# FFT convolution and two expert layers on one core: seven block products for eight in layer two's first product

## Chip, cores and metric

One core of one Trainium2 chip. The metric is the device time of one execution in microseconds. TensorE is PE in the profile (its weight loads PEld), VectorE is DVE, ScalarE ACT, GpSimd POOL, and SP is the engine that issues most DMAs.

## The reference

```python
X = np.fft.rfft(x, axis=1)                                  # x: (2, 3008, 256)
y = np.fft.irfft(X * (filt_r + 1j * filt_i)[None], n=3008, axis=1)
x = y.reshape(6016, 256)
h = x @ moe_w_in                                            # 256 -> 2048
x = np.where(h > 0, h, np.exp(np.minimum(h, 0)) - 1) @ moe_w_out     # 2048 -> 256
h = x @ moe2_w_in
return (h * np.clip(h + 3, 0, 6) / 6) @ moe2_w_out
```

The weights come as 64-bit floats, everything else in 32 bits.

## The kernel before, in words

Features lie on partitions and tokens along the free axis. The convolution is made of small Fourier matrices on PE: for the first sequence ahead of everything else, for the second in between the units of layer one (`PROLOGUE`, `s1`, `mid`, `i1`).

The two layers then work in **units** (layer, token block, hidden block): 12 token blocks of 512, 512, 512, 512, 480 and 480 tokens per sequence, and 16 hidden blocks of 128. A unit has two products. The first (`g1`) goes from 256 features, two blocks of 128, to 128 hidden values; the second (`g2`) goes from those to 256 outputs, two blocks of 128 in two PSUM banks that add up over the 16 hidden blocks. Each product of a 128x128 weight block with a token block is done three times by `mm3` (lines 78 to 81): operands are split in a high part, rounded to fp32r, and the rest, and high by rest, rest by high and high by high are added up in PSUM. So a unit is 4 x 3 = 12 matmuls. Splitting is `split` (lines 74 to 76): an ACT copy (L75) and a DVE subtraction (L76). Between the two products of a layer-two unit stand an ACT relu (L347), a DVE gate (L348) and a split; in layer one it is L341, L342 and L343 and a split.

The loop at lines 587 to 599 is the order of the program: for each unit n first `pre[n]`, then `g1` of unit n, the split of unit n-1, `g2` of unit n-3, and `post[n]`. Units 0 to 191 are layer one, 192 to 383 layer two. `pre` and `post` hold all the side work: the second sequence's convolution, the making of layer two's weights from their 64-bit words (`w_chain`, units 100 to 179, written to memory as `scrw`), and their loading into the buffers of layer one's weights as these come free (`w_load`, on POOL's queue, from unit 179 on). All engines run their queues in order. Layer one's outputs stay in SBUF as `x2`, in the pool `p4` of twenty 4 KB tiles, and are split by `x_split` four units ahead of use. The pool `p2` has twenty 2 KB tiles, PSUM eight banks.

Of the kernel before, what the change touches and what calls it, by code (L numbers as in the profile page):

```python
# [42 lines left out]
def fft_conv_moe_moe2(ctx, tc, xp, fq, sg, cs1, cs1t, cs2, ci2, ci1, ident, w1i, w1o, w2i, w2o, out):  # L43
# [273 lines left out]

    xs, x2, gs, outs = {}, {}, {}, {}

    def x_split(layer, blk, h):  # L320
# [361 lines left out]
```

## Time and profile before

| | |
|---|---|
| median of 3 runs | 1153.73 us (1153.63 to 1154.84) |
| profiled execution | 1154.02 us, of which the span from first to last instruction is 1152.3 us |
| PE, PEld busy | 1136.1 us, 942.7 us |
| DVE, ACT, POOL busy | 760.1 us, 695.7 us, 73.7 us |
| chain that ended last | PE 92% of the span |
| granted TensorE clock | 1.00 |

Busy time of PE counts overlapping matmuls once, and a matmul's duration reaches over the start of the next one. The start of one to the start of the next is what a matmul costs in a stream. For ACT and DVE the same holds on a smaller scale.

### The profile page before, as it was taken

What the parts mean: (1) busy time and instruction counts of PE and PEld (TensorE: products, weight loads), DVE (VectorE), ACT (ScalarE), POOL (GpSimd) and SP (SyncE); (2) the same over time, 40 slices, a digit from 0 to 9 for tenths busy, and PEclk for the clock granted to TensorE, in tenths of its full rate; (3) what the DMA queues carried; (4) which work ended last, traced back from release to release, by engine and by line L of the source; (5) the groups of instructions that cost most, each with busy time, mean ns of one, the idle gap of its engine ahead of it and who ended that gap; (6) DMA issues with size and microseconds to landing.
All of it is one profiled execution on the core that took longest, in us unless ns stands there. A gap on an engine that the chain in (4) does not pass through costs nothing.

```text
span 1152.3 us, 13760 instructions
## 1 busy us (share of the span) xinstructions
PE 1136.1 (99%) x5212; PEld 942.7 (82%) x5212; DVE 760.1 (66%) x1206; ACT 695.7 (60%) x1237; POOL 73.7 (6%) x69
## 2 busy tenths in 40 slices
PE   8899999999999999999999999999999999999998
PEld 5588888788788888888888888888888888888887
DVE  6989998679963788787875555455455555455553
ACT  3477777876676777777776444444444444444443
POOL 3600000024310000000002000000000000000000
PEclk9999999999999999999999999999999999999999
DMA  9991100354522122222226100000000000000000
GB/s 290 290 300 65 42 1 1 110 160 148 165 74 72 37 74 73 74 74 73 81 84 202 54 19 1 19 19 1 19 18 1 18 19 1 19 19 1 19 18 18
DMA packets 50019, 79.75 MB, mean 69 GB/s; under 512 B 4000, under 2 KB 32544, under 8 KB 49952
## 3 DMA queue, kind: packets, MB, share of 16 engines
q1 hardware_dynamic: 46672, 70.14, 19.1%
q0 software_dynamic: 2304, 8.39, 2.4%
q8 instruction: 41, 0.67, 0.2%
q10 hardware_dynamic: 976, 0.34, 0.1%
q14 instruction: 26, 0.21, 0.1%
HBM read 54.87 MB, written 23.99 MB: 68 GB/s over the span
## 4 chain that ended last, share of the span: by engine, by line
PE 92%; DMA 4%; DVE 2%; ACT 0%; SPq 0%; issue 0%; POOL 0%; ACTq 0%; POOLq 0%; DVEq 0%
PE ps L79 30%; PE ps L81 30%; PE ps L80 30%; PE ps L216 2%; DMA raw<-in_w1o 1%; DMA t<-in_fq 1%; DMA t<-in_xp 1%; DVE t L190 1%; DVE t L189 1%; DMA id<-in_ident 1%; POOL t L192 0%; DVE t L76 0%; DMA t<-scr 0%; PE ps L197 0%; ACT t L75 0%
## 5 line engine op out<-in xcount | busy, mean ns | idle before, releaser
L79 PE MATMUL ps<-t,w 128*128 128x512 f32 (+1 forms) x1536 | 593.6, 386 | 0.6 <-DVE t L76 0.5
L81 PE MATMUL ps<-t,w 128*128 128x512 f32 (+1 forms) x1536 | 592.2, 386 | 0.0
L80 PE MATMUL ps<-t,w 128*128 128x512 f32 (+1 forms) x1536 | 592.1, 385 | 0.0
L76 DVE TENSOR_TENSOR t<-t,t 128x512 fp32r<-128x512 f32 (+2 forms) x472 | 329.0, 705 | 9.5 <-ACT t L75 7.6
L79 PEld LDWEIGHTS ps<-t,w 128*128 128x128 f32 x1536 | 288.2, 188 | 56.9 <-PE ps L81 0.9
L81 PEld LDWEIGHTS ps<-t,w 128*128 128x128 f32 x1536 | 288.2, 188 | 55.2
L80 PEld LDWEIGHTS ps<-t,w 128*128 128x128 f32 x1536 | 288.2, 188 | 54.8
L75 ACT ACTIVATE t<-t 128x512 fp32r<-128x512 f32 (+2 forms) x472 | 283.1, 611 | 24.6 <-POOL t L192 24.1
L348 DVE SCALAR_TENSOR_TENSOR t<-t,ps 128x512 f32<-128x512 f32 (+1 forms) x192 | 130.0, 677 | 250.7 <-ACT t L347 250.7
L347 ACT ACTIVATE t<-ps,three 128x512 f32<-128x512 f32 (+1 forms) x192 | 130.6, 680 | 268.6 <-PE ps L81 268.6
L343 DVE SCALAR_TENSOR_TENSOR t<-t,ps 128x512 f32<-128x512 f32 (+1 forms) x192 | 129.5, 675 | 109.3 <-ACT t L342 108.1
L341 ACT ACTIVATE t<-ps 128x512 f32<-128x512 f32 (+1 forms) x192 | 112.3, 585 | 104.5 <-PE ps L81 104.4
L342 ACT ACTIVATE t<-t 128x512 f32<-128x512 f32 (+1 forms) x192 | 119.8, 624 | 6.1
L125 POOL TENSOR_TENSOR t<-t,sg 128x512 f32<-128x512 f32 x24 | 30.3, 1265 | 191.6 <-DMA t<-in_fq 180.7
L192 POOL TENSOR_TENSOR t<-t,t 128x512 f32<-128x512 f32 x24 | 34.9, 1454 | 73.5 <-DVE t L190 48.8
L189 DVE TENSOR_TENSOR t<-ps,t 64x512 f32<-64x512 f32 x48 | 33.1, 689 | 5.7 <-POOL t L125 2.8
L216 PEld LDWEIGHTS ps<-i,t 96*128 96x128 f32 x256 | 31.3, 192 | 3.6 <-issue 2.5
L216 PE MATMUL ps<-i,t 96*128 96x94 f32 x256 | 31.1, 273 | 0.4 <-DMA t<-scr 0.4
L316 POOL DMA_DIRECT2D w<-scrw x16 | 8.6, 540 | 298.8 <-PE ps L81 298.8
L70 ACT ACTIVATE t<-ps 128x512 f32<-128x512 f32 (+12 forms) x51 | 19.4, 421 | 12.4 <-PE ps L149 8.0
L269 DVE SCALAR_TENSOR_TENSOR t<-raw,t 128x512 f32<-128x512 uint32 x32 | 22.3, 697 | 2.0
L263 DVE SCALAR_TENSOR_TENSOR t<-raw,t 128x512 uint32<-128x512 uint32 x32 | 22.7, 710 | 0.4
(54 smaller groups left out, 384.1 us busy)
## 6 DMA issues: line engine op xcount, KB each, us to landing
t<-in_fq SPq DMA_DIRECT2D x24, 512.0 KB, 6.2
scrw<-t SPq DMA_DIRECT2D x16, 512.0 KB, 3.0
w<-scrw POOLq DMA_DIRECT2D x16, 512.0 KB, 4.5
t<-in_xp SPq DMA_DIRECT2D x16, 384.0 KB, 5.2
scr<-t SPq DMA_DIRECT2D x24, 256.0 KB, 2.7
t<-scr SPq DMA_DIRECT2D x16, 384.0 KB, 5.1
raw<-in_w1i SPq DMA_DIRECT2D x18, 256.0 KB, 5.8
raw<-in_w1o SPq DMA_DIRECT2D x18, 256.0 KB, 5.7
```

The lines of the kernel that those rows point to most:

```text
L75: nc.scalar.activation(hi, src, AF.Copy)
L76: nc.vector.tensor_tensor(out=lo, in0=src, in1=_f32(hi), op=ALU.subtract)
L79: nc.tensor.matmul(acc, wh, xl, start=start, stop=False)
L80: nc.tensor.matmul(acc, wl, xh, start=False, stop=False)
L81: nc.tensor.matmul(acc, wh, xh, start=False, stop=stop)
L189: nc.vector.tensor_tensor(out=v[o], in0=acc[a], in1=flat(f[a, 1]), op=ALU.mult)
L216: nc.tensor.matmul(accs[h, jg][:, (j - jg * TG) * TJ : (j - jg * TG + 1) * TJ], vin[b, h, j // 8][:, j % 8, :], mats["i1"], start=True, st ...
L341: nc.scalar.activation(r[:, :n], acc[:, :n], AF.Relu, scale=-1.0)
L342: nc.scalar.activation(r[:, :n], r[:, :n], AF.Exp, scale=-1.0)
L343: nc.vector.scalar_tensor_tensor(out=r[:, :n], in0=r[:, :n], scalar=-1.0, in1=acc[:, :n], op0=ALU.add, op1=ALU.max)
L347: nc.scalar.activation(r[:, :n], acc[:, :n], AF.Relu, bias=three)
L348: nc.vector.scalar_tensor_tensor(out=r[:, :n], in0=r[:, :n], scalar=6.0, in1=acc[:, :n], op0=ALU.min, op1=ALU.mult)
```

## The change

Layer two's first product is taken for two token blocks and two hidden blocks at a time: a product of a 2x2 block matrix of weights (hidden block by feature block) with a 2x2 block matrix of tokens. Eight block products became seven, in Winograd's form of Strassen's scheme. A **group** (p, q) is a pair p of token blocks (six pairs) and a pair q of hidden blocks (eight, "quarters" in what follows). It makes seven products `prod` 1 to 7, each of three matmuls, and eight `second` products of three matmuls.

- The products add up in three banks a, b and c: 1 in a, 2 in b, 6 on top of a, 5 in c, 7 on a, 4 on a, 3 on c. In between ACT copies a to SBUF (`copy`: m1, u2, u3) and DVE adds a copy to a bank (`add`), which gives the hidden blocks (0,0), (1,1) and (0,1); (1,0) is a itself at the end. Then come `relu` (ACT), `gate` (DVE) and `part` (the split), partly in the next group, together with the old group's `second` products. Below, add00 is `add((0, 0))`, and hi00 and lo00 are the ACT and DVE halves of `part((0, 0))`; likewise for the others.
- The weight sums (`w_sums`) are made in layer one, each time two hidden blocks of weights are there: four POOL instructions at once; three units later an ACT copy and a POOL subtraction; five units later a DVE addition and a write to memory. `s_load` brings the sums back on POOL's queue from unit 180 on, behind `w_load`'s.
- The token sums (`x_sums`, four POOL subtractions a pair) and seven splits (`x_part`; four before) are made one pair ahead: for the first pair at units 166 to 188 of layer one, for the others in quarters 2 to 7 of the pair before.
- Layer one's outputs are written to memory (`scrx`) and loaded two blocks at a time (`x2_load`).
- At the end the last group's rest is worked off by itself.

```diff
@@ g2 @@
-        if l == 0:
-            x2[blk] = t
+        nc.sync.dma_start(scrx[blk][:, :, :n], t[:, :, :n])
@@ new: weight sums, called from w_parts for every odd hidden block @@
+    def w_sums(q):
...
+        for out, a, b, op in (
+            (s1, a21, a22, ALU.add), (s2, s1, a11, ALU.subtract),
+            (s3, a11, a21, ALU.subtract), (s4, a12, s2, ALU.subtract),
+        ):
+            nc.gpsimd.tensor_tensor(out=out, in0=a, in1=b, op=op)
...
+        def rounded():
+            nc.scalar.activation(rh, th, AF.Copy)
+            nc.gpsimd.tensor_tensor(out=th, in0=th, in1=_f32(rh), op=ALU.subtract)
+
+        def summed():
+            nc.vector.tensor_tensor(out=rl, in0=th, in1=tl, op=ALU.add)
+            nc.sync.dma_start(scrs[q], _f32(r.rearrange("p q i f -> p (q i f)")))
+
+        pre[now[0] + 3].append(rounded)
+        pre[now[0] + 5].append(summed)
@@ new: token sums and a product @@
+    def x_sums(p, i):
...
+        out, a, b = ((t1, b12, b11), (t2_, b22, t1), (t3, b22, b12), (t4_, b21, t2_))[i]
+        nc.gpsimd.tensor_tensor(out=out, in0=a, in1=b, op=ALU.subtract)
...
+    def prod(p, q, m, acc, start):
...
+        mm3(acc[:, :n], w[:, 0], w[:, 1], x[:, 0, :n], x[:, 1, :n], start, True, True)
@@ new: a group; old is the group before @@
+        a, b, c = bank(), bank(), bank()
+        prod(p, q, 1, a, True)
+        m1 = g.copy(a)
+        prod(p, q, 2, b, True)
+        g.add((0, 0), m1, b)
+        if old:
+            old.part((1, 0))
+            old.relu((0, 1))
+            old.gate((0, 1))
+            old.second((0, 0))
...
+        g.relu((0, 0))
+        if old:
+            old.part((0, 1))
+        g.gate((0, 0))
+        prod(p, q, 6, a, False)
+        u2 = g.copy(a)
+        prod(p, q, 5, c, True)
+        g.part((0, 0))
+        for fn in beside:
+            fn()
+        if old:
+            old.second((1, 1))
...
+        prod(p, q, 7, a, False)
+        u3 = g.copy(a)
+        g.add((1, 1), u3, c)
+        if old:
+            old.second((1, 0))
+            if old.q == NF // 2 - 1:
+                out_evac(old.p, 0)
...
+        g.relu((1, 1))
+        g.gate((1, 1))
+        if old:
+            old.second((0, 1), (0,))
+        prod(p, q, 4, a, False)
+        g.h[1, 0] = a
+        g.relu((1, 0))
+        if (p, q) != (5, NF // 2 - 1):
+            g.gate((1, 0))
+        if old:
+            old.second((0, 1), (1,))
...
+        g.part((1, 1))
+        prod(p, q, 3, c, False)
+        g.add((0, 1), u2, c)
+        return g
@@ the work beside the groups, by quarter; the end @@
+        ahead2 = {
+            1: [(x2_load, 0), (x2_load, 1)], 2: [(x_sums, 0), (x_sums, 1)], 3: [(x_sums, 2), (x_sums, 3)],
+            4: [(x_part, 1), (x_part, 2)], 5: [(x_part, 6), (x_part, 5)], 6: [(x_part, 7), (x_part, 4)],
+            7: [(x_part, 3)],
+        }
...
+        prod(5, NF // 2 - 1, 3, old.c, False)
+        old.add((0, 1), old.u2, old.c)
+        old.relu((0, 1))
+        old.part((1, 1))
+        old.gate((1, 0))
+        old.gate((0, 1))
+        old.part((0, 1))
+        old.part((1, 0))
+        old.second((0, 0))
+        old.second((1, 1))
+        old.second((0, 1))
+        out_evac(old.p, 1)
+        old.second((1, 0))
+        out_evac(old.p, 0)
```

How this moves the instructions, at three places.

PE in the middle of layer two. Before, a unit's second product (banks ps_2110 and ps_2111), then the next unit's first product in a bank of its own:

```order
L79 MATMUL ps_2110_9429<-t2_2115_9448,w_1352_5811 128x480
L80 MATMUL ps_2110_9429<-t2_2114_9447,w_1352_5811 128x480
L81 MATMUL ps_2110_9429<-t2_2114_9447,w_1352_5811 128x480
L79 MATMUL ps_2111_9430<-t2_2115_9448,w_1352_5811 128x480
L80 MATMUL ps_2111_9430<-t2_2114_9447,w_1352_5811 128x480
L81 MATMUL ps_2111_9430<-t2_2114_9447,w_1352_5811 128x480
L79 MATMUL ps_2124_9497<-t4_2076_9266,w_1372_5903 128x480
L80 MATMUL ps_2124_9497<-t4_2075_9265,w_1372_5903 128x480
L81 MATMUL ps_2124_9497<-t4_2075_9265,w_1372_5903 128x480
```

Now, in the middle of a group: product 6 on bank a (ps_2330, in which product 1 lies), product 5 into c (ps_2332), then the old group's second(1,1):

```order
L79 MATMUL ps_2330_9736<-t4_2132_8934,t4_1405_6049 128x512
L80 MATMUL ps_2330_9736<-t4_2132_8934,t4_1405_6049 128x512
L81 MATMUL ps_2330_9736<-t4_2132_8934,t4_1405_6049 128x512
L79 MATMUL ps_2332_9738<-t4_2133_8937,t4_1405_6049 128x512
L80 MATMUL ps_2332_9738<-t4_2133_8937,t4_1405_6049 128x512
L81 MATMUL ps_2332_9738<-t4_2133_8937,t4_1405_6049 128x512
L79 MATMUL ps_2229_9319<-t2_2328_9728,w_1427_6146 128x512
L80 MATMUL ps_2229_9319<-t2_2327_9727,w_1427_6146 128x512
L81 MATMUL ps_2229_9319<-t2_2327_9727,w_1427_6146 128x512
```

The single products now stand between pairs of second products, and a bank is written again after ACT has read it. In all PE has 4827 rows before and 4683 now.

DVE in the middle of layer two. Before, four units' worth, gate and subtraction in turn:

```order
L76 TENSOR_TENSOR t2_1843_8140<-t2_1837_8116,t2_1842_8139 128x512
L348 SCALAR_TENSOR_TENSOR t2_1845_8156<-t2_1845_8156,ps_1844_8149 128x512
L76 TENSOR_TENSOR t2_1847_8160<-t2_1841_8136,t2_1846_8159 128x512
L348 SCALAR_TENSOR_TENSOR t2_1849_8176<-t2_1849_8176,ps_1848_8169 128x512
L76 TENSOR_TENSOR t2_1851_8180<-t2_1845_8156,t2_1850_8179 128x512
L348 SCALAR_TENSOR_TENSOR t2_1853_8196<-t2_1853_8196,ps_1852_8189 128x512
L76 TENSOR_TENSOR t2_1855_8200<-t2_1849_8176,t2_1854_8199 128x512
L348 SCALAR_TENSOR_TENSOR t2_1857_8216<-t2_1857_8216,ps_1856_8209 128x512
```

Now, one group's round: add00, lo10, gate01, lo01, gate00, lo00, add11, gate11, gate10, lo11, add01 (L490 is the addition, L498 the gate):

```order
L490 TENSOR_TENSOR t2_1648_7020<-ps_1645_7010,t2_1647_7015 128x512
L76 TENSOR_TENSOR t2_1650_7023<-t2_1638_6988,t2_1649_7022 128x512
L498 SCALAR_TENSOR_TENSOR t2_1651_7026<-t2_1651_7026,t2_1643_7007 128x512
L76 TENSOR_TENSOR t2_1656_7040<-t2_1651_7026,t2_1655_7039 128x512
L498 SCALAR_TENSOR_TENSOR t2_1654_7037<-t2_1654_7037,t2_1648_7020 128x512
L76 TENSOR_TENSOR t2_1659_7053<-t2_1654_7037,t2_1658_7052 128x512
L490 TENSOR_TENSOR t2_1665_7073<-ps_1646_7011,t2_1664_7071 128x512
L498 SCALAR_TENSOR_TENSOR t2_1666_7081<-t2_1666_7081,t2_1665_7073 128x512
L498 SCALAR_TENSOR_TENSOR t2_1667_7090<-t2_1667_7090,ps_1644_7009 128x512
L76 TENSOR_TENSOR t2_1669_7097<-t2_1666_7081,t2_1668_7096 128x512
L490 TENSOR_TENSOR t2_1670_7103<-ps_1646_7011,t2_1657_7047 128x512
```

Eight rows became eleven, three of them out of PSUM, and at three places a row reads what ACT makes from the row just above it.

DVE at the end of the program. Before:

```order
L348 SCALAR_TENSOR_TENSOR t2_2222_9976<-t2_2222_9976,ps_2221_9969 128x480
L76 TENSOR_TENSOR t2_2224_9980<-t2_2218_9956,t2_2223_9979 128x480
L348 SCALAR_TENSOR_TENSOR t2_2226_9996<-t2_2226_9996,ps_2225_9989 128x480
L76 TENSOR_TENSOR t2_2228_10000<-t2_2222_9976,t2_2227_9999 128x480
L76 TENSOR_TENSOR t2_2230_10010<-t2_2226_9996,t2_2229_10009 128x480
L381 TENSOR_SCALAR t4_2231_10031<-ps_2180_9762 128x240
```

Now (add01, lo11, gate10, gate01, lo01, lo10, and the two copies out):

```order
L490 TENSOR_TENSOR t2_2548_10634<-ps_2532_10555,t2_2541_10589 128x480
L76 TENSOR_TENSOR t2_2551_10639<-t2_2546_10617,t2_2550_10638 128x480
L498 SCALAR_TENSOR_TENSOR t2_2547_10626<-t2_2547_10626,ps_2530_10553 128x480
L498 SCALAR_TENSOR_TENSOR t2_2549_10636<-t2_2549_10636,t2_2548_10634 128x480
L76 TENSOR_TENSOR t2_2553_10645<-t2_2549_10636,t2_2552_10644 128x480
L76 TENSOR_TENSOR t2_2555_10649<-t2_2547_10626,t2_2554_10648 128x480
L474 TENSOR_SCALAR t2_2557_10673<-ps_2417_10072 128x480
L474 TENSOR_SCALAR t2_2559_10685<-ps_2409_10045 128x480
```

Six DVE rows now stand behind the last first-product, where two stood before.

## Rows read from the trace of the kernel before

**Rows 1.** The page, part 1: busy us (share) xinstructions of each engine.

```profile
PE 1136.1 (99%) x5212; PEld 942.7 (82%) x5212; DVE 760.1 (66%) x1206; ACT 695.7 (60%) x1237; POOL 73.7 (6%) x69
```

**Rows 2.** Windows: PE, PEld, DVE, ACT, POOL busy (x), clock, DMA share, GB/s.

```profile
100.00:125.00 25.00, 25.00 (x112) 20.72 (x111) 23.02 (x40) 19.22 (x35) 0.00 (x0) 1.00 0.06 17
...
450.00:475.00 25.00, 25.00 (x112) 20.69 (x111) 20.49 (x35) 19.17 (x35) 0.00 (x0) 1.00 0.25 85
...
631.00:1148.00 517.00, 516.90 (x2316) 433.91 (x2314) 264.00 (x419) 246.52 (x421) 1.58 (x3) 1.00 0.05 16
```

**Rows 3.** Timeline, ACT in layer two: start us, us, engine, line [idle before <-releaser].

```profile
701.38 0.69 ACT L347 ACTIVATE t<-ps,three 128x512 f32<-128x512 f32 x1 [1.51 <-PE ps L81]
701.96 0.62 ACT L75 ACTIVATE t<-t 128x512 fp32r<-128x512 f32 x1
704.10 0.69 ACT L347 ACTIVATE t<-ps,three 128x512 f32<-128x512 f32 x1 [1.51 <-PE ps L81]
...
1137.54 0.66 ACT L347 ACTIVATE t<-ps,three 128x480 f32<-128x480 f32 x1 [1.45 <-PE ps L81]
...
1140.14 0.66 ACT L347 ACTIVATE t<-ps,three 128x480 f32<-128x480 f32 x1 [1.45 <-PE ps L81]
```

**Rows 4.** Groups by line and shape: busy us, mean ns of one, idle before.

```profile
L341 ACT ACTIVATE t<-ps 128x512 f32<-128x512 f32 x128 | 76.1, 595 | 73.0 <-PE ps L81 72.9
...
L190 DVE TENSOR_TENSOR t<-ps,t 128x512 f32<-128x512 f32 x24 | 16.6, 692 | 0.5
```

**Rows 5.** Timeline, DVE and ACT with queued work, 100 to 106 us.

```profile
104.54 0.69 DVE L263 SCALAR_TENSOR_TENSOR t<-raw,t 128x512 uint32<-128x512 uint32 x1
105.14 0.69 DVE L281 TENSOR_TENSOR t<-t,w 128x512 f32<-128x512 f32 x1
...
100.45 0.61 ACT L75 ACTIVATE t<-t 128x512 fp32r<-128x512 f32 x1
100.97 0.62 ACT L279 ACTIVATE w<-t 128x512 fp32r<-128x512 f32 x1
```

**Rows 6.** Timeline of layer two: handovers between engines, and DVE at 480 columns.

```profile
700.95 0.39 PE L81 MATMUL ps<-t,w 128*128 128x512 f32 x1
...
702.10 0.69 DVE L348 SCALAR_TENSOR_TENSOR t<-t,ps 128x512 f32<-128x512 f32 x1 [1.43 <-ACT t L347]
...
1133.03 0.65 DVE L348 SCALAR_TENSOR_TENSOR t<-t,ps 128x480 f32<-128x480 f32 x1 [1.38 <-ACT t L347]
1133.60 0.65 DVE L76 TENSOR_TENSOR t<-t,t 128x480 fp32r<-128x480 f32 x1
...
1143.43 0.65 DVE L348 SCALAR_TENSOR_TENSOR t<-t,ps 128x480 f32<-128x480 f32 x1 [1.38 <-ACT t L347]
...
1144.12 0.60 ACT L75 ACTIVATE t<-t 128x480 fp32r<-128x480 f32 x1 [0.23 <-DVE t L348]
```

**Rows 7.** Timeline, PE going on after a wait for DVE, 308 us.

```profile
308.10 0.50 PE L79 MATMUL ps<-t,s_h 128*128 128x512 f32 x1 [0.86 <-DVE t L76]
...
308.44 0.40 PE L80 MATMUL ps<-t,s_l 128*128 128x512 f32 x1
```

**Rows 8.** Timeline, POOL and DVE side by side, 257 to 261 us.

```profile
257.02 1.52 POOL L192 TENSOR_TENSOR t<-t,t 128x512 f32<-128x512 f32 x1 [4.11 <-DVE t L190]
258.50 1.49 POOL L125 TENSOR_TENSOR t<-t,sg 128x512 f32<-128x512 f32 x1
...
257.90 1.19 DVE L76 TENSOR_TENSOR t<-t,t 128x512 fp32r<-128x512 f32 x1
259.24 1.29 DVE L76 TENSOR_TENSOR t<-t,t 128x512 fp32r<-128x512 f32 x1 [0.15 <-ACT t L75]
```

**Rows 9.** Timeline, the end: the last matmul and the last DMA issue.

```profile
1147.52 0.38 PE L81 MATMUL ps<-t,w 128*128 128x480 f32 x1
...
1148.77 0.34 SPq L382 DMA_DIRECT2D out<-t  x1
```

**Rows 10.** The page, part 6: a DMA issue, count, KB each, us to landing.

```profile
w<-scrw POOLq DMA_DIRECT2D x16, 512.0 KB, 4.5
```

More of the change, by code (lines that the diff above doesn't have):

```diff
@@ new lines, in prod, with second @@
+    def prod(p, q, m, acc, start):
+        n = BLOCKS[2 * p % 6]
+        if m in (1, 2):
+            w = wts[1, 2 * q][:, :, (m - 1) * P : m * P]
+        elif m == 4:
+            w = wts[1, 2 * q + 1][:, :, P : 2 * P]
+        else:
+            w = sums[q][:, :, {5: 0, 6: 1, 7: 2, 3: 3}[m], :]
+        x = ops[p, m]
+        mm3(acc[:, :n], w[:, 0], w[:, 1], x[:, 0, :n], x[:, 1, :n], start, True, True)
+    def second(p, q, i, k, d, g):
+        n = BLOCKS[2 * p % 6]
+        if (p, k, d) not in outs:
+            outs[p, k, d] = bank()
+        w = wts[1, 2 * q + i]
+        s = slice(256 + d * P, 256 + (d + 1) * P)
+        mm3(
+            outs[p, k, d][:, :n], w[:, 0, s], w[:, 1, s], g[0][:, :n], g[1][:, :n],
+            q == 0 and i == k, q == NF // 2 - 1 and i != k,
+        )
@@ new lines, in out_evac, with __init__, copy, add @@
+    def out_evac(p, k):
+        blk = 2 * p + k
+        n = BLOCKS[blk % 6]
+        t0 = (blk // 6) * S + EDGES[blk % 6]
+        for d in range(2):
+            o, t = outs.pop((p, k, d)), t2([P, 512])
+            if d == 0:
+                nc.scalar.activation(t[:, :n], o[:, :n], AF.Copy, scale=1.0 / 6.0)
+            else:
+                nc.vector.tensor_scalar_mul(t[:, :n], o[:, :n], 1.0 / 6.0)
+            nc.sync.dma_start(out[d * P : (d + 1) * P, t0 : t0 + n], t[:, :n])
+    class Group:
+        def __init__(self, p, q):
+            self.p, self.q, self.n = p, q, BLOCKS[2 * p % 6]
+            self.h, self.g = {}, {}
+        def copy(self, bank_):
+            t = t2([P, 512])
+            nc.scalar.activation(t[:, : self.n], bank_[:, : self.n], AF.Copy)
+            return t
+        def add(self, key, u, bank_):
+            n = self.n
+            self.h[key] = t2([P, 512])
+            nc.vector.tensor_tensor(out=self.h[key][:, :n], in0=bank_[:, :n], in1=u[:, :n], op=ALU.add)
+        def relu(self, key):
+            self.g[key] = t2([P, 512])
+            nc.scalar.activation(self.g[key][:, : self.n], self.h[key][:, : self.n], AF.Relu, bias=three)
+        def gate(self, key):
+            n, r = self.n, self.g[key]
+            nc.vector.scalar_tensor_tensor(
+                out=r[:, :n], in0=r[:, :n], scalar=6.0, in1=self.h.pop(key)[:, :n], op0=ALU.min, op1=ALU.mult
+            )
+        def part(self, key):
+            n, g = self.n, self.g[key]
+            gh, gl = t2([P, 512], F32R), t2([P, 512], F32R)
+            split(gh[:, :n], gl[:, :n], g[:, :n])
+            self.g[key] = gh, gl
+        def second(self, key, d=(0, 1)):
+            for d_ in d:
+                second(self.p, self.q, key[0], key[1], d_, self.g[key])
@@ L585, in fft_conv_moe_moe2 @@
                 split_mat("s1")
+        NU = len(units)
         for n, u in enumerate(units):
+            now[0] = n
             for fn in pre[n]:
@@ L596, in fft_conv_moe_moe2, with rest, run @@
                 fn()
-        g_split(units[-1])
-        for u in units[-SKEW:]:
-            g2(u)
+        def rest(n):
+            def run():
+                if n == NU:
+                    g_split(units[-1])
+                g2(units[n - SKEW])
+                for fn in post[n]:
+                    fn()
+            return run
+        old = None
+        ahead2 = {
[3 more added lines that the diff above has]
+        }
+        for p in range(6):
+            for q in range(NF // 2):
+                beside = [
+                    (lambda fn=fn, i=i: fn(p + 1, i)) for fn, i in (ahead2.get(q, ()) if p < 5 else ())
+                ]
+                old = group(p, q, old, [rest(NU + i) for i in range(3)], beside)
+        prod(5, NF // 2 - 1, 3, old.c, False)
[9 more added lines that the diff above has]
+        old.second((0, 1))
+        out_evac(old.p, 1)
+        old.second((1, 0))
+        out_evac(old.p, 0)
 def _tables():
```

102 lines of the change are left out of this document (71 added, 31 removed).

## The prediction

> **What bounds the kernel now.** I read the busy totals first: PE works 1136.1 of 1152.3 us [rows 1]. Then the windows by stage: from 631 to 1148 us, which is all of layer two (192 units), PE is busy 516.90 of 517.00 us at a granted clock of 1.00, while DVE works 264.00 us and ACT 246.52 us [rows 2]. So a matmul taken out of layer two is worth its pitch in full, as long as DVE and ACT keep up. That pitch isn't the 386 ns duration, since matmuls overlap. It comes from the timeline: L347 runs once a unit and follows PE, and it starts at 701.38 and 704.10, so a unit of 12 matmuls takes 2.72 us at 512 columns (0.2267 us each); at 480 columns 1137.54 to 1140.14, 2.60 us (0.2167 us each) [rows 3].
>
> The profiled execution took 1154.02 us, its span 1152.3 us. The median of the three runs is 1153.73 us, 0.29 us lower. I sum against 1154.02 and take 0.29 off at the end. Such a measurement can tell about 0.2% (2.3 us) from no change.
>
> **The matmuls removed.** A group (two token blocks, two hidden blocks) needs 45 matmuls where four units needed 48. There are 48 groups, 32 of them 512 wide and 16 of them 480 wide: 96 x 0.2267 + 48 x 0.2167 = 21.76 + 10.40 = **32.16 us off**. PE's rows fall by just these 144, from 4827 to 4683.
>
> **What must hide for that.** A group now takes PE 45 x 0.2267 = 10.20 us (480: 9.75). In it DVE issues 11 instructions (3 additions out of PSUM, 4 gates, 4 low halves; 8 before) and ACT 11 (3 copies out of PSUM, 4 relus, 4 high halves; 8 before). The nearest rows: L341, PSUM to SBUF, 595 ns for a copy, and L190, PSUM and SBUF to SBUF, 692 ns for an addition [rows 4]. Queued instructions start closer than they last: on DVE 104.54 to 105.14, 0.60 us apart; on ACT 100.45 to 100.97, 0.52 us [rows 5]. ACT: 3 x 0.48 + 4 x 0.58 + 4 x 0.52 = 5.8 us of 10.2, at most 7.4 if each took 0.67.
>
> DVE is the tighter one, because its queue is in order and at three places its next instruction needs an ACT result made from the instruction just before: lo01 (after gate01), lo00 (after gate00), gate11 (after add11). A handover costs little: DVE's L348 starts at 702.10 where ACT's 0.69 us from 701.38 end at 702.07; ACT's L75 starts at 1144.12 where DVE's 0.65 us from 1143.43 end at 1144.08 [rows 3, 6]. So from such a DVE instruction to the next one pass 0.69 + 0.04 + 0.62 + 0.03 = 1.38 us (1.45 with a relu) in place of 0.60. **DVE's round** is 11 x 0.60 + 0.78 + 0.78 + 0.85 = 9.01 us against PE's 10.20: 1.19 us of room. At 480 (0.57 apart, 1133.03 to 1133.60 [rows 6]) it is 8.56 against 9.75. PE's nearest due time is M7, which needs the copy u2. M7's slot is 8 x 0.68 = 5.44 us into the group. M2 lands at 1.56 (the last matmul's 0.39 us from 700.95 ends 0.16 us after the next one's slot, and ACT starts 0.04 us later [rows 3, 6]). Then add00 starts at 1.56, lo10 at 2.16, gate01 at 2.76 and ends at 3.45, hi01 starts at 3.49, u2 at 4.01 and is done at 4.60: 0.84 us early. In plain groups I take nothing.
>
> **Groups with other work beside them.** For each of five pairs, the next pair's operands are split in quarters 4 to 7 (two, two, two and one splits). Two splits add 2 x 0.60 us to the round: 10.21 against 10.20; one makes 9.61. The five groups that also empty the output banks have the same 10.21. On paper 0.01 us each; I take 0.1 us for 20 such groups, since a stop also costs PE a slow restart (0.34 us from 308.10 to the next matmul, not 0.23 [rows 7]): 2.0 us. Bounds: 0, and each split uncovered with its whole chain (0.62 + 0.69 + 0.07 = 1.38 us), a round of 11.77, 1.57 x 15 = 24 us.
>
> **POOL's operand sums** (L432 of the changed kernel): four subtractions a pair, two in quarter 2, two in quarter 3, for five pairs in layer two. POOL itself is idle there, but DVE's L76 took 1.19 and 1.29 us beside POOL's L192 and L125, for its usual 0.69 [rows 8]: some 0.55 us more. In quarter 3 POOL's two buffers come free with add01 and add00, so lo10 and gate01 both meet it: 1.1 to 1.3 us later, against u2's 0.84, so 0.3 to 0.5 us lost. In quarter 2 they come free with the old group's last matmuls and with lo11, and only lo11 and lo10 meet POOL: some 0.6 us, within the 0.84. I take 0.4 us in five groups: 2.0 us. Bounds: 0, and DVE shut out for both POOL instructions in all ten groups: 9.01 + 2.9 - 10.20 = 1.7, times 10 = 17 us. The Trainium skill (SBUF — State Buffer, section Who interferes with whom) states that a DVE instruction with two SBUF inputs and a GpSimd instruction that reads SBUF exclude each other for a whole instruction, which speaks against putting these sums on POOL. The two L76 end at 259.09 and 260.53, each about 0.55 us after POOL's record (258.54, 259.99), so this trace agrees; by the rule alone the term would be the 17 us, by the row's 0.55 it is 2.
>
> **The end.** The last group has nobody to hide behind. Counted from the end of its last matmul slot, at 480 columns: add01 0.20 to 0.85, relu01 to 1.54, hi11 from 1.43 to 2.02, lo11 from 2.05 to 2.70; PE has second(0,0) until 1.30, so it stands 1.46 us before second(1,1), which then runs to 4.06. DVE goes on with gate10 at 2.62 and gate01 at 3.19, hi01 ends at 4.47, lo01 at 5.15: PE stands 1.15 us more before second(0,1). With two slow restarts: **2.8 us added**; 2 to 4 as bounds. The final copy and its DMA issue took 1.25 us from the last matmul's start (1147.52 to 1148.77 [rows 9]); two full-width copies side by side and two issues take about the same: 0.
>
> **Layer one.** The weight sums add, for each of eight q's, one ACT copy, five POOL instructions and one DVE addition, over ten units (27.2 us), between units 110 and 184. In the fullest window there DVE works 20.49 of 25 us [rows 2], so 22.3 of 27.2; the addition (0.60) and five meetings with POOL (5 x 0.55) make 25.7 (94%). At 100 to 125 us DVE carried 92% beside a full PE [rows 2]: 0. Without this cover 8 x 3.4 = 27 us. The 12 writes and 12 loads of layer one's outputs replace tiles held in SBUF. The slowest like it, 512 KB on POOL's queue, lands in 4.5 us [rows 10], and they are due tens of units later: 0. SP's and POOL's queues carry eight sums' writes and eight loads more; POOL's loads stand behind the weight loads, which wait for PE one unit at a time, and the last sum is due seven groups later: 0.
>
> **Sum:** 1154.02 - 32.16 + 2.0 + 2.0 + 2.8 = 1128.7; less 0.29: **1128.4 us**.
>
> **Rivals.**
> - *Everything hides.* For it: DVE's round has 1.19 us free and PE runs seamlessly in layer two [rows 2]. Only the end is paid: 1124.4 us.
> - *The operand splits don't fit.* If one of two splits falls into a place where DVE waits, the round is 9.01 + 0.60 + 1.38 = 10.99, 0.79 us lost in each of 15 groups, 11.9 in place of 2.0: 1138.3 us. For it: the margin is 0.01 us. Against: the splits depend on nothing in the group.
> - *POOL shuts DVE out.* A mechanism of this kernel by rows 8: DVE stands for both of POOL's 1.45 us in each of ten groups, 17 us in place of 2: 1143.4 us. For it: both L76 in the rows ended after POOL. Against: they lost 0.5 to 0.6 us, not 1.5. The rule of the Trainium skill named above would give this.
> - *The copies run behind PE; slower than before.* M6, M7 and M4 add into a bank that ACT has just copied, and the copy stands in ACT's queue behind a chain from DVE. If u2 comes d late in every group, each loses d - 0.84; this decides against the change from d = 0.84 + 0.68 = 1.52 us on. Were lo10, gate01 and add00 all of the length that DVE showed beside POOL (1.24), d would be 1.75, 0.9 us lost in 48 groups, 43.7 us: 1168 us. Against: in layer two POOL is beside 10 groups of 48, and add00 reads PSUM.
> - *Nothing is removed:* excluded by PE's 144 fewer rows.
>
> **How the numbers follow.** Forecast (1125.5 to 1132) 0.45, everything hides (1122.5 to 1125.5) 0.2, splits 0.14, POOL 0.1, partly uncovered layer one or a mix near no change 0.06, slower 0.05. The range 1122.5 to 1140 holds the first three, 0.79. Faster by over 0.2%: 0.93; within: 0.02; slower: 0.05.
>
> **What would show it.** PE matmuls down by 144; plain groups of layer two at 10.2 and 9.75 us; PE's idle time in layer two a few us, in quarters 3 to 7 and the last 10 us; DVE some 9 of each 10 us, L76 lengthened where L432 runs; the clock still 1.00. Wrong if plain groups take over 10.4 us, if layer one ends later than 631 us, or if the waits name ACT's copies in every group.

## The result and the profile after

The changed kernel takes **1135.09 us** in the median of four runs (1131.76 to 1140.04), the one before 1153.68 beside it: a ratio of 0.984, 95% interval 0.980 to 0.988. The profiled execution of the changed kernel took 1133.89 us, 20.1 less than the profiled one of before (1154.02); the two traces are compared below. The page, part 1, of the changed kernel:

```profile
PE 1109.5 (98%) x5068; PEld 915.1 (81%) x5068; DVE 885.8 (78%) x1376; ACT 793.5 (70%) x1406; POOL 151.1 (13%) x141
```

Against [rows 1], PE has 144 rows fewer (the page counts 5212 and 5068, where the prediction has 4827 and 4683; the difference is the same), and DVE 170 and ACT 169 more. Where the 20.1 us come from, read from the starts of the first and the last matmul of each stage:

| us | before | after | difference |
|---|---|---|---|
| to the first matmul of layer one | 73.3 | 75.7 | +2.4 |
| layer one | 556.0 | 556.6 | +0.7 |
| layer two, first to last matmul start | 518.2 | 495.7 | -22.5 |
| last matmul start to the end of the span | 4.7 | 4.0 | -0.7 |

**Layer two.** Its windows in the changed kernel (PE, PEld, DVE, ACT, POOL busy, clock, DMA share, GB/s), up to the end's last 12 us and those:

```profile
632.00:1118.00 486.00, 482.45 (x2147) 401.39 (x2146) 366.99 (x570) 334.17 (x572) 29.48 (x24) 1.00 0.09 29
1118.00:1130.00 12.00, 8.16 (x36) 6.07 (x34) 5.65 (x9) 4.62 (x8) 0.00 (x0) 1.00 0.17 62
```

PE stands 3.55 us in 486 at the full clock of 2.4 GHz, and 2.3 more before its last matmul ends at 1128.46. That is not yet all that is lost: matmuls overlap, and one that starts up to 0.16 us late (0.39 less 0.23) leaves no idle time. The starts show it all, by the first matmul of each group. For the second pair, quarters 1, 2, 3 and 4 begin at:

```profile
724.06 0.39 PE L79 MATMUL ps<-t,w 128*128 128x512 f32 x1
...
734.26 0.39 PE L79 MATMUL ps<-t,w 128*128 128x512 f32 x1
...
744.46 0.39 PE L79 MATMUL ps<-t,w 128*128 128x512 f32 x1
...
755.56 0.39 PE L79 MATMUL ps<-t,w 128*128 128x512 f32 x1
```

Quarters 1 and 2 take 10.20 us each, which is 45 x 0.2267; quarter 3 takes 11.10. The table has what each quarter took beyond 45 pitches, summed over the six pairs, for this kernel and for the experiments below (the sixth pair, which has no side work, loses under 0.1 in all). "End" is the time from first to last start of the last 24 matmuls, less 23 x 0.2167 = 4.98 us.

| us lost in quarter | 0 | 1 | 2 | 3 | 4 | 5 | 6 | 7 | end | layer two |
|---|---|---|---|---|---|---|---|---|---|---|
| changed kernel | 0.0 | 0.1 | 0.0 | **4.95** | 0.0 | 0.1 | 1.2 | 0.2 | 2.86 | 495.7 |
| changed kernel again | 0.0 | 0.1 | 0.0 | 4.99 | 0.0 | 0.1 | 1.1 | 0.1 | 4.41 | 497.1 |
| sums on DVE | 0.0 | 0.1 | 0.0 | 0.1 | 2.0 | 1.2 | 1.5 | 0.2 | 2.85 | 494.2 |
| POOL, one a quarter | 0.1 | 2.5 | 0.0 | 0.0 | 4.5 | 1.2 | 1.5 | 0.1 | 2.85 | 499.1 |
| end reordered | 0.0 | 0.1 | 0.0 | 4.92 | 0.0 | 0.0 | 1.2 | 0.1 | 0.44 | 493.1 |
| end, sums on DVE spread | 0.0 | 0.1 | 0.0 | 0.0 | 0.2 | 0.1 | 1.2 | 0.1 | 0.47 | 488.6 |
| end, sums on POOL spread | 0.1 | 2.5 | 0.0 | 0.1 | 3.2 | 0.0 | 0.3 | 0.0 | 0.47 | 493.1 |
| no sums after the first pair | 0.0 | 0.1 | 0.0 | 0.0 | 0.0 | 0.3 | 1.0 | 0.1 | 2.86 | 490.7 |

**Quarter 3** of the first pair in the timeline of the changed kernel. L432 are POOL's token sums, DVE's L490 is add00 (add01 stands just before it), the first L76 lo10, the first L498 gate01; L75 is hi01, L484 the copy u2, and L79 the first matmul of product 7:

```profile
663.04 1.30 POOL L432 TENSOR_TENSOR t<-t 128x512 f32<-128x512 f32 x1 [8.95 <-ACT t L484]
663.07 0.69 DVE L490 TENSOR_TENSOR t<-ps,t 128x512 f32<-128x512 f32 x1 [0.18 <-PE ps L81]
...
663.68 1.21 DVE L76 TENSOR_TENSOR t<-t,t 128x512 fp32r<-128x512 f32 x1
...
664.30 1.73 POOL L432 TENSOR_TENSOR t<-t,t 128x512 f32<-128x512 f32 x1
...
664.81 1.77 DVE L498 SCALAR_TENSOR_TENSOR t<-t,t 128x512 f32<-128x512 f32 x1
...
666.61 0.63 ACT L75 ACTIVATE t<-t 128x512 fp32r<-128x512 f32 x1 [1.95 <-DVE t L498]
...
667.15 0.58 ACT L484 ACTIVATE t<-ps 128x512 f32<-128x512 f32 x1
...
667.78 0.50 PE L79 MATMUL ps<-t,t 128*128 128x512 f32 x1 [0.74 <-ACT t L484]
...
668.12 0.39 PE L80 MATMUL ps<-t,t 128*128 128x512 f32 x1
```

Every DVE instruction with two SBUF inputs that begins during a POOL sum ends 0.5 to 0.55 us after POOL's record in layer two, whenever it began (664.34 and 664.89; 666.03 and 666.58). add00, which reads PSUM, runs its usual 0.69 beside POOL. lo10 is 0.52 longer, gate01 1.08, together 1.6 us against u2's room of 0.84: ACT reaches u2 late, and product 7 with it. The stop of 0.74 and the slow restart (0.34 for 0.23) make the 0.9 of a group. In quarter 2 the same two sums cost PE nothing; DVE beside them:

```profile
650.80 0.69 DVE L498 SCALAR_TENSOR_TENSOR t<-t,ps 128x512 f32<-128x512 f32 x1 [0.18 <-ACT t L494]
651.40 1.24 DVE L76 TENSOR_TENSOR t<-t,t 128x512 fp32r<-128x512 f32 x1
...
653.76 0.87 DVE L76 TENSOR_TENSOR t<-t,t 128x512 fp32r<-128x512 f32 x1
```

lo11 and lo10 are longer by 0.55 and 0.18, and that fits.

**Two splits a quarter** cost nothing at first, but DVE falls behind. add01 of the first pair, by quarters 4, 5 and 6 (which begin at 672.68, 682.88 and 693.10; a row x2 is add01 and add00, and starts with add01):

```profile
673.50 1.49 DVE L490 TENSOR_TENSOR t<-ps,t 128x512 f32<-128x512 f32 x2
...
684.18 1.28 DVE L490 TENSOR_TENSOR t<-ps,t 128x512 f32<-128x512 f32 x2
...
694.65 1.28 DVE L490 TENSOR_TENSOR t<-ps,t 128x512 f32<-128x512 f32 x2
```

It starts 0.82, 1.30 and 1.55 us into its quarter. So the two splits of quarter 4 make DVE's round some 0.5 us too long, not 0.01, and quarter 6 is the first in which PE waits (0.3 us in this pair).

**The end**: the two stops of PE in the last group.

```profile
1121.32 0.38 PE L81 MATMUL ps<-t,w 128*128 128x480 f32 x1
1123.06 0.49 PE L79 MATMUL ps<-t,w 128*128 128x480 f32 x1 [1.36 <-DVE t L76]
...
1125.59 0.48 PE L79 MATMUL ps<-t,w 128*128 128x480 f32 x1 [0.94 <-DVE t L76]
...
1128.08 0.38 PE L81 MATMUL ps<-t,w 128*128 128x480 f32 x1
```

**Layer one.** One stop of PE there that the kernel before has not, behind a low half (L76) that met a token sum of the first pair:

```profile
566.30 1.68 POOL L432 TENSOR_TENSOR t<-t 128x512 f32<-128x512 f32 x1 [3.09 <-DVE t L283]
...
567.30 1.19 DVE L76 TENSOR_TENSOR t<-t,t 128x480 fp32r<-128x480 f32 x1
...
568.55 0.48 PE L79 MATMUL ps<-t,w 128*128 128x480 f32 x1 [0.41 <-DVE t L76]
```

**The start** has the same program in both kernels. Windows of the kernel before, then of the changed one:

```profile
30.00:35.00 5.00, 4.79 (x32) 3.48 (x30) 4.89 (x8) 2.93 (x6) 4.16 (x5) 1.00 1.04 394
35.00:40.00 5.00, 2.68 (x16) 1.94 (x17) 4.49 (x5) 1.74 (x4) 3.64 (x3) 1.00 1.10 358
40.00:50.00 10.00, 9.70 (x36) 4.67 (x35) 9.11 (x14) 3.66 (x7) 4.81 (x4) 1.00 0.79 190
```

```profile
30.00:35.00 5.00, 5.00 (x41) 4.52 (x40) 4.89 (x7) 3.33 (x5) 4.17 (x5) 1.00 1.05 397
35.00:40.00 5.00, 2.48 (x12) 1.36 (x11) 4.93 (x7) 1.70 (x3) 4.76 (x4) 0.93 1.08 364
40.00:50.00 10.00, 9.86 (x32) 4.90 (x31) 7.01 (x13) 3.58 (x6) 2.59 (x3) 0.86 0.66 179
```

The granted clock fell here after a stretch in which PE worked 2.48 of 5 us; in the kernel before, with 2.68 of 5, it did not. But 1.1 of the 2.4 us came before that: POOL waited longer for a load of the filter (`in_fq`), first before and then in the changed kernel, and PE waited for POOL.

```profile
24.66 1.04 POOL L125 TENSOR_TENSOR t<-t,sg 128x512 f32<-128x512 f32 x1 [2.40 <-DMA t<-in_fq]
```

```profile
25.80 1.04 POOL L125 TENSOR_TENSOR t<-t,sg 128x512 f32<-128x512 f32 x1 [3.60 <-DMA t<-in_fq]
```

The changed kernel with its end reordered (experiment 5), the same up to its last group, began layer one at 73.2 us with the clock at 1.00 up to there. So the change by itself does not bring a later start.

### The profile page after: what moved, and what is told of

Its sections match the earlier page's. It is cut to its first block, busy times and chain, and to the rows that moved or that the text cites. A ratio compares the mean times of both kernels' runs of the same rounds, so it can differ in the third digit from the quotient of the medians.

```text
span 1132.1 us, 14291 instructions
## 1 busy us (share of the span) xinstructions
PE 1109.5 (98%) x5068; PEld 915.1 (81%) x5068; DVE 885.8 (78%) x1376; ACT 793.5 (70%) x1406; POOL 151.1 (13%) x141
## 4 chain that ended last, share of the span: by engine, by line
PE 86%; DVE 7%; DMA 3%; ACT 2%; issue 2%; POOL 0%; SPq 0%; ACTq 0%; DVEq 0%; POOLq 0%
PE ps L79 28%; PE ps L81 27%; PE ps L80 27%; PE ps L216 2%; DVE t L76 2%; DVE t L498 1%; DVE t L189 1%; DMA t<-in_fq 1%; DMA t<-in_xp 1%; ACT t L75 1%; DVE t L190 1%; DVE t L490 1%; DMA id<-in_ident 0%; DVE t L386 0%; POOL t L192 0%
## 5 line engine op out<-in xcount | busy, mean ns | idle before, releaser
L79 PE MATMUL ps<-t,w 128*128 128x512 f32 (+1 forms) x1296 | 502.2, 387 | 3.4 <-DVE t L76 3.1
L81 PE MATMUL ps<-t,w 128*128 128x512 f32 (+1 forms) x1296 | 499.9, 386 | 0.0
L80 PE MATMUL ps<-t,w 128*128 128x512 f32 (+1 forms) x1296 | 499.8, 386 | 0.0
L76 DVE TENSOR_TENSOR t<-t,t 128x512 fp32r<-128x512 f32 (+2 forms) x490 | 351.4, 728 | 79.3 <-ACT t L75 75.9
L75 ACT ACTIVATE t<-t 128x512 fp32r<-128x512 f32 (+2 forms) x490 | 293.6, 613 | 98.4 <-DVE t L498 72.8
L79 PEld LDWEIGHTS ps<-t,w 128*128 128x128 f32 x1296 | 243.2, 188 | 54.4 <-DVE t L76 3.9
L81 PEld LDWEIGHTS ps<-t,w 128*128 128x128 f32 x1296 | 243.1, 188 | 46.9
L80 PEld LDWEIGHTS ps<-t,w 128*128 128x128 f32 x1296 | 243.2, 188 | 45.8
L386 DVE SCALAR_TENSOR_TENSOR t<-t,ps 128x512 f32<-128x512 f32 (+1 forms) x192 | 129.3, 674 | 91.5 <-ACT t L385 90.4
L384 ACT ACTIVATE t<-ps 128x512 f32<-128x512 f32 (+1 forms) x192 | 112.3, 585 | 96.9 <-PE ps L81 96.6
L498 DVE SCALAR_TENSOR_TENSOR t<-t,t 128x512 f32<-128x512 f32 (+1 forms) x144 | 102.7, 713 | 33.7 <-ACT t L494 33.5
L494 ACT ACTIVATE t<-t,three 128x512 f32<-128x512 f32 (+1 forms) x144 | 97.7, 710 | 44.5 <-DVE t L490 43.2
L484 ACT ACTIVATE t<-ps 128x512 f32<-128x512 f32 (+1 forms) x144 | 83.5, 580 | 25.3 <-PE ps L81 23.4
L490 DVE TENSOR_TENSOR t<-ps,t 128x512 f32<-128x512 f32 (+1 forms) x144 | 94.5, 674 | 5.6 <-PE ps L81 2.7
L432 POOL TENSOR_TENSOR t<-t,t 128x512 f32<-128x512 f32 (+1 forms) x18 | 25.5, 1418 | 283.8 <-PE ps L81 278.3
L79 PE MATMUL ps<-t,t 128*128 128x512 f32 (+1 forms) x120 | 46.9, 391 | 3.5 <-ACT t L484 3.5
L80 PE MATMUL ps<-t,t 128*128 128x512 f32 (+1 forms) x120 | 46.3, 386 | 0.0
L81 PE MATMUL ps<-t,t 128*128 128x512 f32 (+1 forms) x120 | 46.3, 386 | 0.0
L498 DVE SCALAR_TENSOR_TENSOR t<-t,ps 128x512 f32<-128x512 f32 (+1 forms) x48 | 32.3, 674 | 12.2 <-ACT t L494 12.2
```

Source lines behind the costliest of these rows:

```text
L75: nc.scalar.activation(hi, src, AF.Copy)
L76: nc.vector.tensor_tensor(out=lo, in0=src, in1=_f32(hi), op=ALU.subtract)
L79: nc.tensor.matmul(acc, wh, xl, start=start, stop=False, skip_group_check=more)
L80: nc.tensor.matmul(acc, wl, xh, start=False, stop=False, skip_group_check=more)
L81: nc.tensor.matmul(acc, wh, xh, start=False, stop=stop, skip_group_check=more)
L386: nc.vector.scalar_tensor_tensor(out=r[:, :n], in0=r[:, :n], scalar=-1.0, in1=acc[:, :n], op0=ALU.add, op1=ALU.max)
```

## The experiments

The theory after the comparison: layer two loses the time that POOL's sums take from DVE in quarter 3 (4.95 us), the end's two stops (2.86) and a little beside the splits (1.5); the start's 2.4 us vary from run to run. Rivals: what is lost in quarter 3 comes from the amount of side work, whoever does it; or it comes from memory traffic or buffers.

**1. The changed kernel again**, unchanged.

> The changed kernel once more, beside the others, for the spread of its times and for where that spread arises. Its four runs lay from 1131.76 to 1140.04 us with granted clocks of 1.000 to 0.990, those of before from 1152.86 to 1154.84. Theory A (the start varies, layer two doesn't): layer two from first to last matmul start again 496 us within 1, quarter 3 again about 11.1 us a group where the others take 10.2; unit 0's first matmul anywhere from 73.8 to some 80 us. Theory B (layer two itself varies): its length differs by several us from 496.

Measured: 1135.19 us median (1133.22 to 1140.98), ratio 0.984 (0.982 to 0.986). Quarter 3 lost 4.99 us and quarter 6 1.1, so these losses are the program's. The profiled run was its slowest, 1140.98 us. Windows of it in the start and in the end:

```profile
70.00:80.00 10.00, 10.00 (x48) 10.00 (x48) 6.23 (x11) 6.56 (x17) 0.00 (x0) 0.50 0.92 304
80.00:90.00 10.00, 9.97 (x36) 7.64 (x36) 5.57 (x10) 6.97 (x13) 0.00 (x0) 0.83 0.87 276
...
1132.00:1136.00 4.00, 3.54 (x11) 2.60 (x9) 1.08 (x2) 1.14 (x2) 0.00 (x0) 0.66 0.32 123
```

At the 1.2 GHz level (0.50) PE is full and late: layer one began at 79.6 us, and the end took 1.5 us more, so that layer two came out at 497.1 us, just outside the 1 us expected. Most of the runs' spread goes with the clock, which fell in the first 100 us and, here, after the end's stops too.

**2. The sums of the second to sixth pair on DVE.**

```diff
-        nc.gpsimd.tensor_tensor(out=out, in0=a, in1=b, op=ALU.subtract)
+        eng = nc.vector if p else nc.gpsimd
+        eng.tensor_tensor(out=out, in0=a, in1=b, op=ALU.subtract)
```

> Layer two's token sums on DVE in place of POOL. Theory A (in quarter 3 POOL's two subtractions shut DVE out of lo10 and gate01, so the copy u2 comes late and product 7 waits): quarter 3 falls from 11.1 to 10.2 or 10.3 us a group (two more DVE instructions make its round 10.21), five groups, 4 to 5 us less in all. Rival B (quarter 3 stops for a free buffer of the pool p2, four of which the sums hold): quarter 3 stays at 11.1, and quarters 2 and 3 lose more with 1.2 us of DVE work added to each.

Measured: 1134.3 us median (1130.76 to 1145.88). Quarter 3's 4.95 us are gone, as expected, but quarter 4 has 2.0 and quarter 5 1.2 that it had not: layer two gains 1.5 us only. Two sums, two sums, two splits and two splits in quarters 2 to 5 each make DVE later, and the lag is handed on from group to group. (By the sum of the prediction they ask 1.20 us of a room of 1.19; the room is smaller, as add01's starts showed above.)

**3. POOL's sums one a quarter.**

```diff
-            1: [(x2_load, 0), (x2_load, 1)], 2: [(x_sums, 0), (x_sums, 1)], 3: [(x_sums, 2), (x_sums, 3)],
-            4: [(x_part, 1), (x_part, 2)], 5: ...
+            0: [(x2_load, 0), (x2_load, 1)], 1: [(x_sums, 0)], 2: [(x_sums, 1)], 3: [(x_sums, 2)],
+            4: [(x_part, 1), (x_part, 2), (x_sums, 3)], 5: ...
```

> The token sums stay on POOL, but one in each of quarters 1 to 4 in place of two in 2 and two in 3; the loads a quarter earlier. Theory A (each POOL subtraction holds up one or two DVE instructions by 0.4 to 1.1 us, and only two in a row outlast the 0.84 us by which u2 is early): quarter 3 falls to 10.2 to 10.4, quarter 4, which has two splits too, rises to 10.3 to 10.8; 3 to 4 us less in all. Rival B (buffers): no change in quarter 3, since the four tiles are held longer.

A miss: 1137.05 us median (1134.38 to 1144.48), and layer two 3.3 us longer. One sum costs nothing in quarters 2 and 3, but 0.5 us a pair in quarter 1 and 0.9 in quarter 4. Either quarter 4 loses it because two splits stand there too, or because of what the sum meets there; experiment 6 tells these apart.

**4. The change's side work alone**, in the kernel with eight products.

```diff
-        if l == 0:
-            x2[blk] = t
+        nc.sync.dma_start(scrx[blk][:, :, :n], t[:, :, :n])
...
+    def x2_load(blk):
...
+            if f % 2:
+                w_sums(f // 2)
```

> The kernel before, with eight products, but with the change's work in layer one: outputs written to memory and loaded again, and the weight sums made and written (not read). Theory A (this work hides; the 2.4 us later start seen in one profile is the start's own variation): the time of before within 1 us, layer two starts within 1 us of where it starts in before counted from unit 0. Rival B (the side work or its memory slows layer one or the start): 1 to 4 us over before in the median, and a start as late as the changed kernel's in most runs.

Measured: 1156.55 us median (1152.45 to 1168.97 in twelve runs) beside 1155.38 of before, ratio 1.001 (0.999 to 1.004). That is 1.2 us over, which the expectation gave to rival B, and in the profiled run layer one took 558.1 us where before took 556.0. But these 2.1 us lie in its first 28 us, where the clock was low:

```profile
70.00:80.00 10.00, 10.00 (x50) 9.42 (x49) 6.16 (x11) 5.44 (x14) 0.00 (x0) 0.58 0.91 311
80.00:90.00 10.00, 9.98 (x41) 7.76 (x40) 7.58 (x13) 8.72 (x16) 0.00 (x0) 0.91 1.02 342
```

From one and the same matmul behind that (2286 matmuls of lines 79 to 81 ahead of layer two's first) to layer two, it took 530.2 us in before and here:

```profile
99.08 0.39 PE L79 MATMUL ps<-t,w 128*128 128x512 f32 x1
...
629.28 0.39 PE L79 MATMUL ps<-t,w 128*128 128x512 f32 x1
```

```profile
105.08 0.39 PE L79 MATMUL ps<-t,w 128*128 128x512 f32 x1
...
635.29 0.39 PE L79 MATMUL ps<-t,w 128*128 128x512 f32 x1
```

Layer two took 518.2 us in both. So weight sums and the way through memory are hidden, behind the start at least; the loading of the sums and the token sums are not in this kernel. Six of its twelve runs had a mean clock of 0.995 or less, and two of the seventeen of before.

**5. The end reordered**: each last split as early as its queue allows.

```diff
         prod(5, NF // 2 - 1, 3, old.c, False)
         old.add((0, 1), old.u2, old.c)
+        old.part((1, 0))
         old.relu((0, 1))
-        old.part((1, 1))
-        old.gate((1, 0))
         old.gate((0, 1))
         old.part((0, 1))
-        old.part((1, 0))
         old.second((0, 0))
         old.second((1, 1))
-        old.second((0, 1))
-        out_evac(old.p, 1)
         old.second((1, 0))
         out_evac(old.p, 0)
+        old.second((0, 1))
+        out_evac(old.p, 1)
```

(gate10 and lo11 now stand in the group, ahead of product 3.)

> The changed kernel with another order in its last group alone: DVE goes gate10, lo11, add01, lo10, gate01, lo01, and PE second(0,0), second(1,1), second(1,0), the first block's output copies, then second(0,1). Counted matmuls and all else are the same. Theory (the 2.86 us of the end are two stops behind DVE's and ACT's chain for add01): lo11 is ready before second(0,0) ends, so the first stop goes; of the second, some 0.3 us stay before second(0,1). From first to last start of the last 24 matmuls 7.84 us become about 5.5 (4.98 is the least), 2.3 us less in layer two; median 1132 to 1133 where the changed kernel has 1135. Rival (the end's length is the clock's: PE stops there anyway after a long full stretch): the 7.84 stay within 0.5 us.

Measured: 1131.15 us median (1128.81 to 1134.12), ratio 0.977 (0.974 to 0.981). The end's 7.84 us are 5.42. One stop is left:

```profile
1121.82 0.48 PE L79 MATMUL ps<-t,w 128*128 128x480 f32 x1 [0.19 <-DVE t L76]
```

**6 and 7. End reordered, sums spread**, once on DVE and once on POOL. The first pair's four sums stand three units apart (163, 166, 169, 172), and no quarter has more than two extra instructions (in the second kernel the last line is `eng = nc.gpsimd`). In both a sum's tile is taken when the sum is made, not all four at once:

```diff
+            0: [(x2_load, 0), (x2_load, 1)], 1: [(x_sums, 0)], 2: [(x_sums, 1), (x_part, 1)],
+            3: [(x_sums, 2), (x_part, 2)], 4: [(x_sums, 3)], 5: [(x_part, 6), (x_part, 5)],
+            6: [(x_part, 7), (x_part, 3)], 7: [(x_part, 4)],
...
+        eng = nc.vector if p else nc.gpsimd
```

> The kernel with the end reordered, and the operand sums of the second to sixth pair as DVE subtractions, spread with the splits so that no quarter has more than two extra DVE instructions: loads in quarter 0, one sum in 1, a sum and a split in 2 and in 3, one sum in 4, two splits in 5 and in 6, one in 7. The first pair's four sums stay on POOL, three units apart. Theory (DVE's round has 1.19 us of room, and what does not fit is carried into the next quarter, as happened when two sums stood in quarters 2 and 3 ahead of the splits): each round is at most 10.21 of 10.20 us, so quarter 3's 4.95 us go and nothing comes in their place but 0.1 to 0.3 us a quarter: all quarters together lose 1 to 3 us where the changed kernel lost 6.5; layer two from 495.7 to about 489 to 490 us; median 1127 to 1129. Rival (rounds of 10.2 do not fit in PE's 10.2, lag builds up over quarters 2 to 6): 1 us a pair in quarters 3 to 6, 5 us, and no better than with the end reordered alone.

> As the kernel before it, with the sums on POOL, one in each of quarters 1 to 4, in quarters 2 and 3 beside one split, in 4 beside none. Theory (a POOL subtraction costs DVE's queue its whole length only where an SBUF instruction of DVE falls on it; one alone cost nothing in quarters 2 and 3, 0.5 us in 1 and 0.8 to 1.2 in 4 beside two splits): with the splits moved away from quarter 4, quarter 4 loses 0 to 0.3 us a pair, quarter 1 some 0.5, together 3 to 4 us with the splits' quarters; median 1129 to 1131, between the kernel with the end reordered and the one with the sums on DVE. Rival (what counts is the amount of DVE work, not POOL's reads): POOL's sums leave DVE the two extra instructions less, so this one is the fastest, 1 to 2 us below the sums on DVE.

With the sums on **DVE**: **1126.6 us** median (1125.08 to 1140.14), ratio 0.975 (0.971 to 0.980), the fastest of all. Window of layer two without the end, and the sums' groups on DVE:

```profile
630.00:1113.00 483.00, 482.94 (x2155) 403.01 (x2154) 367.99 (x591) 335.14 (x574) 2.11 (x4) 1.00 0.09 31
```

```profile
L432 DVE TENSOR_TENSOR t<-t,t 128x512 f32<-128x512 f32 (+1 forms) x15 | 10.1, 672 | 0.0
L432 DVE TENSOR_TENSOR t<-t 128x512 f32<-128x512 f32 (+1 forms) x5 | 3.4, 671 | 0.0
```

PE stands 0.06 us in 483 there; by the starts the quarters lose 1.8 us, most of it in quarter 6. Twenty sums of 0.67 us on DVE cost less than twenty of 1.4 us on POOL. Layer one, with the first pair's sums apart, took 556.0 us, and 556.2 in the POOL kernel, where the four kernels with those sums in four units running and layer one at full clock took 556.6 to 556.8. Counted from the same matmul as in experiment 4, it is 530.3 us in these two and 530.9 to 531.0 in the six others with the token sums.

With the sums on **POOL**: 1131.73 us (1128.53 to 1144.76), above the range given; quarter 4 still loses 3.2 us, though no split is there. Its rows for quarter 4 and then quarter 1 of the first pair:

```profile
676.50 1.60 POOL L432 TENSOR_TENSOR t<-t,t 128x512 f32<-128x512 f32 x1 [9.95 <-DVE t L491]
...
676.87 1.78 DVE L499 SCALAR_TENSOR_TENSOR t<-t,t 128x512 f32<-128x512 f32 x1
...
679.86 0.50 PE L79 MATMUL ps<-t,t 128*128 128x512 f32 x1 [0.36 <-ACT t L485]
```

```profile
643.11 1.30 POOL L432 TENSOR_TENSOR t<-t,t 128x512 f32<-128x512 f32 x1 [0.80 <-DVE t L499]
...
643.73 1.23 DVE L76 TENSOR_TENSOR t<-t,t 128x512 fp32r<-128x512 f32 x1
...
648.56 0.50 PE L79 MATMUL ps<-t,zt 128*128 128x512 f32 x1 [0.28 <-ACT t L485]
```

In quarter 4 the sum starts just ahead of gate01, which stands 1.1 us. In quarter 1 it lengthens lo11 by 0.55 us only; but lo11 starts there 1.05 us into its group (642.68), where a plain one starts 0.16 in, because DVE's L412 empties an output bank just before. So of experiment 3's two readings it is mostly the place (3.2 of its 4.5 us stay without the splits): which DVE instruction the sum falls on, and how late DVE is then.

**8. No sums after the first pair.**

```diff
+        if p:
+            xt[p] = [xb[p, k][:, c] for k in range(2) for c in range(2)]
+            return
         if i == 0:
             xt[p] = [t2([P, 512]) for _ in range(4)]
```

> The changed kernel with the operand sums of the second to sixth pair left out: the splits for products 4 to 7 read the loaded blocks themselves, so POOL does nothing in layer two, and its output differs. All else stands. It prices the term of POOL's sums by itself. Theory (the 4.95 us of the five quarter-3 groups are POOL's): they fall to 0.1, the 1.2 us of quarter 6 and the end's 2.86 stay; layer two 495.7 to about 490.8 us, median 1130. Rival (quarter 3 loses its 1 us through the loads or buffers that come free there, whoever computes): at least 2 of the 4.95 us stay.

Measured: 1133.6 us median (1127.45 to 1142.24; two of six runs at a clock of 0.983), 3.6 over the median expected. Layer two took 490.7 us as expected, and quarter 3 lost nothing:

```profile
632.00:1118.00 486.00, 485.94 (x2170) 406.01 (x2168) 359.11 (x574) 336.89 (x575) 2.45 (x5) 1.00 0.09 31
```

PE's 3.55 us of standing are 0.06. The loads are as they were, so they have no part in the 4.95 us. The sums' four buffers are not taken in this kernel; but experiment 2 took them just as before, with the sums on DVE, and quarter 3 lost 0.1. So the 4.95 us are what POOL's sums take from DVE.

## Why the prediction came out as it did

The 1135.1 us lie inside the range, 6.7 us above the forecast. Step by step:

- **The matmuls removed** (-32.16): right. PE's rows fell by 144 and plain groups take 10.20 and 9.75 us.
- **DVE's round and the splits** (+2.0): near in size, by luck. Plain groups lose nothing, and the quarters with splits or output copies lost 1.5 us together (quarters 0 and 4 to 7). But the round of 10.21 against 10.20 was wrong: two splits made DVE some 0.5 us late (0.82 to 1.30 by add01's starts), not 0.01, and "0.1 us for 20 such groups" hid it. Nearly all of the loss fell in quarter 6, the third in a row with two splits. What one group's queue cannot hold is late in the next.
- **POOL's operand sums** (+2.0): this is the step that failed in size. I let lo10 and gate01 be 0.55 us longer each, which gave 1.1 to 1.3 us, and took 0.4 us a group. gate01 stood 1.08, because the second sum had begun just before it; 1.6 less 0.84 is the stop of 0.76, and the restart brings it to 0.9 to 1.07 a group: **4.95 us in place of 2.0**. Place, chain and number of groups were right, quarter 2 at nothing too. The 0.55 us of [rows 8] is how much later than POOL the DVE instruction ends, not how much longer it takes: that depends on when it began. By the rule of the Trainium skill (SBUF — State Buffer, section Who interferes with whom) the two exclude each other for a whole instruction. The trace agrees (gate01 1.77 beside a sum of 1.73, and add00 and the gate that read PSUM untouched), but not with the 17 us that I drew from it, since only in quarter 3 is the wait longer than the room.
- **The end** (+2.8): right, 2.86, with stops of PE's queue of 1.52 and 1.11 us where I had 1.46 and 1.15. The cost was one of order: it is 0.44 when reordered. The final copy at 0 was 0.7 too high: from last matmul to the span's end 4.0 us, before 4.7.
- **Layer one** (0): 0.66 measured. Weight sums and memory traffic cost nothing that shows (experiment 4); the row at 568.55 and the 0.4 to 0.7 us that the kernels with spread sums save put this on the first pair's token sums, which I had not counted there. One sign of being wrong did show: layer one ended after 631 us (layer two's first matmul at 632.35). That was the start's 2.4 us and these 0.66, not the weight sums for which the sign was meant. The loads that I took to land in 4.5 us at most took 4.7 to 9.0 (512 KB of `scrs` on POOL's queue), without a wait that shows.
- **What no step had**: the start, +2.4 us in the profiled run, from a later load (1.1) and the clock, and 1.2 more between this run and the median. The one run at a clock of 1.000 took 1131.8. That the median still lies inside the range is owed to the range's width, not to a term for this.
- **DVE some 9 of each 10 us**, as a sign, did not hold: it was busy 366.99 of 486 us, 7.6 of each 10. The 9.01 count DVE's waits for ACT too.

In sum: 1128.7 + 2.95 (POOL) + 2.4 (start) + 0.66 (layer one) - 0.5 (splits) - 0.7 (last copy) + 0.06 (end) = 1133.6, where 1133.89 was measured; 0.3 stays without a place.

**The rivals.** *Everything hides* falls by quarter 3. *The splits don't fit* falls in the changed kernel, but experiment 2 made it true with four full quarters in a row. *POOL shuts DVE out* had the right mechanism and too many groups. *The copies run behind PE* shows in five groups of 48, not in all.

Open: whether the changed kernels make the clock's falls in the start likelier. On one chip their runs with seven products were at 0.995 or less in 10 of 17, those of before in 2 of 17; on the other in 12 of 24 and 5 of 11. The kernel of experiment 4, with eight products and the side work, was there in 6 of 12, so if there is a difference, the seven products are not what makes it. The start's program is the same in all, and no run told the cause apart.

## What to carry to other kernels

Where an in-order queue has room of one or two instructions, count the side work of neighbouring stretches together, since lag is handed on. Before giving work to an engine because it is idle, look at which instruction of the busy engine will stand beside it: here 0.67 us in DVE's own queue was cheaper than 1.4 us on an idle POOL. Where the last stage has no work left to hide behind, order each queue by what the next engine needs first; that alone was worth 2.4 us.
